# Moving part of the score sums and the output scaling between VectorE and ScalarE in a two-layer decode kernel

## The chip, the cores and the metric

The kernel runs on one core of one Trainium2 chip. The metric is the device time of one execution in microseconds (us). Every time that is read from a trace comes from one profiled execution and is counted from the start of its span. The engines are written as in the profile: PE is TensorE (PEld its weight loads), DVE is VectorE, ACT is ScalarE, POOL is GpSimd, and SPq is the queue of SyncE, from which nearly all loads are issued.

## The reference

One new token for each of two batch rows goes through an attention layer and a gated feed-forward layer, and then through both once more with the same weights and the same cache:

```python
B, Sq, D = 2, 1, 448;  H, Sk, Dh = 16, 4096, 256;  F = 1792
def _A_ref(x, k_cache, v_cache, wq, wo):
    q = (x @ wq).reshape(B, Sq, H, Dh).transpose(0, 2, 1, 3)
    scores = einsum("bhqd,bhkd->bhqk", q, k_cache) * (Dh ** -0.5)
    o = einsum("bhqk,bhkd->bhqd", softmax(scores), v_cache)
    return o.transpose(0, 2, 1, 3).reshape(B, Sq, H * Dh) @ wo
def _B_ref(x, W_gate, W_up, W_down):
    gate = x @ W_gate;  up = x @ W_up
    return (relu(gate) * up) @ W_down
x = x + _A_ref(layernorm(x), ...);  x = x + _B_ref(layernorm(x), ...)
x = x + _A_ref(layernorm(x), ...);  x = x + _B_ref(layernorm(x), ...)
```

All of it is float32. Keys and values of one head and one batch row are 4 MB each, so a pass over the cache reads nearly 270 MB.

## The kernel before

**Units and passes.** A unit is one head for one batch row, so a pass of attention has 32 units, numbered `u` from 0 to 31. The kernel has two passes, `attention(first, keep)` and `attention(second, ...)`, and behind each the feed-forward layer, `ffn(False)` and `ffn(True)`. A unit's keys are 128 partitions of 32 key rows ("tiles" `t`) of 256 numbers each, cut into four chunks `c` of 8 tiles; its values are cut in the same way.

**Loads and slots.** All weights, keys and values pass through one SBUF buffer, `arena`, of 27 slots of 1 MB. The list of loads is written out at the start. `pump` issues the next load from SyncE when a slot (or a block of 4 or 8 slots) is free; `release`, called behind the last reader of a slot, frees it and calls `pump`. Loads are issued in the list's order, so a load that has no slot holds up all behind it. In the middle of a pass one load brings 8 MB: the keys of unit `u` with the values of unit `u-1`. At the end of the first pass 20 chunks, the keys of units 29, 30 and 31 and the values of 30 and 31, together with one more chunk of values and one head's weights, stay in their slots, because the second pass begins with these units. While they stay, the remaining loads (7 of `w_in`, 4 of `w_out`, then the second pass) go through the five slots that are left.

**Scores.** The scores of a unit are products of its keys with the query, summed over 256 numbers. There are three ways of making them, and the first two appear in this case's edits.

- A block (`score_block`): VectorE multiplies all 32 tiles in place with one instruction (L378) and sums them with one (L386). Where `shared` is `CT` (8), ScalarE sums the first 8 tiles (L382) and VectorE the other 24. That is so for unit 0 of the first pass and for units from `ALONE` (25) on in both passes, and for three blocks early in the second pass.
- Kept keys (`score` with `kept`, units 29, 30 and 31 of the first pass): VectorE takes tile after tile with one instruction that multiplies and sums (L418, SCALAR_TENSOR_TENSOR). The products go to `junk`, a part of `down`, since the keys are wanted again.
- The rest, chunk by chunk, shared between VectorE and ScalarE (L409 to L418). Units 30 and 31 of the second pass are among these.

**Around the scores.** For each unit come the greatest score of a partition (`softmax_max`, L427 on VectorE and L429 on GpSimd), the exponentials (`softmax_exp`, L434 and L437 on ScalarE), the product with the values (`weigh`, L462 on TensorE), and the sum of its partial results in two steps: `out_copy` (L475, ScalarE) and `out_add` (L478, VectorE). `out_turn` (L488, TensorE) transposes the result, `out_keep` (L501, VectorE) scales it by the reciprocal of the softmax's sum for two units at once, and `project` (L511, TensorE) multiplies by `wo`. The order of a pass is the loop at the end of `attention`: in round `u` stand the scores of unit `u`, the weighing of unit `u-1` and the output of unit `u-2`. Each engine takes its instructions in that order. `query(u + 1)`, which makes the queries of two units, stands behind `project` in the rounds of odd `u`. For units 30 and 31 of the first pass the query stays in PSUM (`pq`), and TensorE makes it in round 29.

**The end.** In `ffn(True)` the output has four blocks of columns `c`, made from the four loads of `w_out`. The first three are gathered in `y_left`, copied by VectorE as one tile of 384 columns (L702) and written out by SyncE (L703); the last 64 columns go through `y_end` (L708 to L711) and are written by ScalarE's queue.

## Time and profile before

| | us |
|---|---|
| median of 3 runs (lowest, highest) | 1320.69 (1320.47, 1320.93) |
| the profiled execution, its own time | 1320.27 |
| its span | 1318.5 |
| busy in the span: DVE | 1081.6 (82%) |
| busy: PE | 553.7 (42%) |
| busy: ACT | 195.6 (15%) |
| busy: POOL | 269.0 (20%) |
| moved by DMA | 563.16 MB, 427 GB/s on average |

The time outside the span is 1320.27 - 1318.5 = 1.8 us. Shares of busy time are averages over stages: the middle of a pass, the turn from the first pass through `ffn(False)` to the second (about 570 to 760 us), and the end (from about 1220 us). In a row of the timeline stand start, duration, engine, line, operation, what is written and read, and in brackets how long the engine had been idle before it and what ended that.

### The profile page before, as it was taken

To read this page: it belongs to the slowest core of one execution; us is meant where nothing else is said; L and a number is where in the kernel's file an instruction comes from. 1 tells how busy PE (TensorE), PEld (TensorE's weight loads), DVE (VectorE), ACT (ScalarE), POOL (GpSimd) and SP (SyncE) were. 2 spreads that over 40 slices of the span, in tenths; PEclk is the share of its full clock that TensorE was granted. 3 is DMA by queue.
4 is the path that set the end of the run, shared out by engine and by line. 5 is a ranking of instruction groups with operands and counts; after the bars stand their busy time and mean duration, and the time that the engine had idled before them with its cause. 6 is when DMAs were issued, how large, how long until landed. Compare 5 with 4: busy or idle time off the path is not lost.

```text
span 1318.5 us, 9085 instructions
## 1 busy us (share of the span) xinstructions
PE 553.7 (42%) x3276; PEld 190.6 (14%) x3276; DVE 1081.6 (82%) x780; ACT 195.6 (15%) x776; POOL 269.0 (20%) x192
## 2 busy tenths in 40 slices
PE   2243342433434324345585444242433424434348
PEld 2011010110111101112141111110111101101113
DVE  4989888898888988888729987798888988877892
ACT  2100000000000000212026513000000000012241
POOL 0002003322133220321001153030123331230210
PEclk9675666656667667666697777666767667666679
DMA  9999999999999999999999999999999999999998
GB/s 408 435 430 429 432 428 437 432 436 434 417 445 435 430 430 426 445 418 430 421 405 416 431 430 435 438 432 430 432 431 436 433 428 436 429 432 425 427 425 334
DMA packets 22665, 563.16 MB, mean 427 GB/s; under 512 B 2520, under 2 KB 2652, under 8 KB 9564
## 3 DMA queue, kind: packets, MB, share of 16 engines
q1 hardware_dynamic: 22612, 562.57, 99.5%
q8 instruction: 26, 0.43, 0.1%
q14 instruction: 19, 0.16, 0.0%
q10 hardware_dynamic: 8, 0.00, 0.0%
HBM read 562.56 MB, written 0.00 MB: 427 GB/s over the span
## 4 chain that ended last, share of the span: by engine, by line
DMA 55%; DVE 32%; PE 7%; POOL 2%; issue 2%; ACT 1%; DVEq 0%; SPq 0%; POOLq 0%; ACTq 0%
DMA arena<-in_vk_dram 54%; DVE arena L378 12%; DVE scores L386 11%; DVE arena L409 3%; DVE down L418 2%; PE po L462 2%; POOL top L429 2%; DVE arena L418 2%; DMA arena<-in_w_out_dram 1%; DVE row L478 1%; PE small L488 1%; PE acc L511 1%; DVE scores L415 1%; ACT arena L411 1%; PE pf L576 1%
## 5 line engine op out<-in xcount | busy, mean ns | idle before, releaser
L378 DVE TENSOR_TENSOR arena<-arena 128x8192 f32<-128x8192 f32 x51 | 443.3, 8692 | 111.0 <-DMA arena<-in_vk_dram 110.9
L386 DVE TENSOR_REDUCE scores<-arena 128x32 f32<-128x8192 f32 (+1 forms) x53 | 431.8, 8148 | 0.0
L488 PE MATMUL small<-ones,row 128*128 128x1 f32 x256 | 62.0, 346 | 686.3 <-DVE row L478 686.3
L462 PE MATMUL po<-arena,probs 128*2 128x512 f32 x2048 | 303.1, 734 | 10.3 <-DMA arena<-in_vk_dram 6.6
L429 POOL PARTITION_ALL_REDUCE top<-mx x64 | 64.6, 1009 | 645.8 <-DVE mx L427 645.8
L443 POOL PARTITION_ALL_REDUCE total<-rs x64 | 176.1, 2752 | 61.3 <-ACT probs L437 60.3
L488 PEld LDWEIGHTS small<-ones,row 128*128 128x128 f32 x256 | 56.5, 308 | 748.9 <-DVE row L478 748.9
L434 ACT ACTIVATE nm<-top,nsr 128x1 f32<-128x1 f32 x64 | 18.8, 294 | 612.4 <-POOL top L429 612.4
L354 POOL PARTITION_BROADCAST arena<-arena x58 | 27.6, 545 | 300.6 <-ACT arena L350 300.6
L462 PEld LDWEIGHTS po<-arena,probs 128*2 128x2 f32 x2048 | 54.8, 96 | 198.3 <-issue 191.2
L338 PE MATMUL pq<-arena,xs 128*33 128x256 f32 x174 | 70.6, 571 | 14.1 <-DMA arena<-in_w_head_dram 14.1
L511 PE MATMUL acc<-arena,oT 128*2 128x448 f32 x128 | 50.9, 894 | 32.1 <-DVE oT L501 32.1
L350 ACT ACTIVATE arena<-pq 33x256 f32<-33x256 f32 x29 | 10.9, 377 | 321.7 <-PE pq L342 321.7
L382 ACT ACTIVATE arena<-arena 128x256 f32<-128x256 f32 x104 | 41.7, 402 | 86.2 <-DVE arena L378 86.2
L478 DVE SCALAR_TENSOR_TENSOR row<-po,lead,row 128x256 f32<-128x256 f32 x64 | 30.7, 479 | 25.8 <-ACT row L475 25.4
L411 ACT ACTIVATE arena<-arena 128x256 f32<-128x256 f32 x117 | 47.1, 404 | 20.4 <-DVE arena L409 20.1
L409 DVE TENSOR_TENSOR arena<-arena 128x1024 f32<-128x1024 f32 (+1 forms) x24 | 42.0, 1748 | 0.0
L338 PEld LDWEIGHTS pq<-arena,xs 128*33 128x33 f32 x174 | 25.3, 162 | 81.3 <-issue 66.7
L475 ACT ACTIVATE row<-po,lead 128x256 f32<-128x256 f32 x64 | 29.1, 455 | 21.2 <-PE po L462 21.2
L418 DVE SCALAR_TENSOR_TENSOR down<-arena,pq 128x256 f32<-128x256 f32 x64 | 26.9, 420 | 5.4 <-DMA arena<-in_vk_dram 3.4
L501 DVE TENSOR_TENSOR oT<-small,ri 128x4 f32<-128x4 f32 x32 | 5.1, 161 | 29.0 <-PE small L488 29.0
L437 ACT ACTIVATE probs<-scores,nm,sr 128x32 f32<-128x32 f32 x64 | 26.4, 413 | 2.1
(145 smaller groups left out, 359.0 us busy)
## 6 DMA issues: line engine op xcount, KB each, us to landing
arena<-in_vk_dram SPq DMA_DIRECT2D x16, 4096.0 KB, 40.0
arena<-in_w_head_dram SPq DMA_DIRECT2D x31, 896.0 KB, 30.9
arena<-in_vk_dram SPq DMA_DIRECT2D x27, 1024.0 KB, 14.9
arena<-in_vk_dram SPq DMA_DIRECT2D x12, 2048.0 KB, 38.5
arena<-in_w_in_dram SPq DMA_DIRECT2D x14, 896.0 KB, 26.2
arena<-in_w_out_dram SPq DMA_DIRECT2D x5, 896.0 KB, 8.9
arena<-in_vk_dram SPq DMA_DIRECT2D x47, 43.4
arena<-in_w_out_dram SPq DMA_DIRECT2D x1, 512.0 KB, 17.3
```

Of the source, the lines that this page charges most:

```text
L338: nc.tensor.matmul(q, xs[:, c, :], w[:, c * DH : (c + 1) * DH], start=(c == 0), stop=False)
L378: nc.vector.tensor_mul(kt, kt, q_of[u][:, None, :].to_broadcast([P, NT, DH]))
L386: nc.vector.reduce_sum(s_of[u][:, shared:], kt[:, shared:, :], axis=AX.X)
L409: nc.vector.tensor_mul(some, some, q_of[u][:, None, :].to_broadcast([P, whole, DH]))
L411: nc.scalar.activation(kt[:, t, :], kt[:, t, :], AF.Copy, accum_out=found[:, t : t + 1])
L418: nc.vector.scalar_tensor_tensor(junk if kept else kt[:, t, :], kt[:, t, :], 1.0, q_of[u], op0=ALU.mult, op1=ALU.mult, accum_out=found[:, ...
L429: nc.gpsimd.partition_all_reduce(mx_of[u], mx, P, RED.max)
L443: nc.gpsimd.partition_all_reduce(total[:, b : b + 1], rs, P, RED.add)
L462: nc.tensor.matmul(po_of[u][32 * t : 32 * t + 2, :], p_of[u][:, n : n + 2], vt[:, 2 * t * DH : (2 * t + 2) * DH], start=(c == 0), stop=(c ...
L478: nc.vector.scalar_tensor_tensor(row[:, :DH], po_of.pop(u)[:, DH:], lead[:, 1:2], row[:, :DH], op0=ALU.mult, op1=ALU.add,)
L488: nc.tensor.matmul(pT_of[u - u % 2][:, c, b : b + 1], row[:, c * P : (c + 1) * P], ones, start=True, stop=True,)
L511: nc.tensor.matmul(acc[at : at + B], oT_of[h][:, c, :], wo[:, c * D : (c + 1) * D], start=(n < 3), stop=(n >= n_u - 3),)
```

## The change

- In `score_block` ScalarE no longer takes 8 tiles at the end of a pass: VectorE sums all 32 tiles of units 25 to 28 of the first pass and 25 to 29 of the second.
- Of kept keys, tiles with odd `t` are multiplied by VectorE into `product` (the second half of `row`, one buffer for all of them) and summed by ScalarE. Even tiles stay as they were.
- `out_keep`'s multiplication for two units on VectorE becomes `out_scale`, an ACTIVATE for each unit on ScalarE. The one for an even unit is issued behind the reciprocal, that for an odd unit where `out_keep` stands.
- In `ffn(True)` the third block of output columns has its own PSUM tile, `y_third`. VectorE copies the first two blocks (256 columns), ScalarE the third.

```diff
-ALONE = 25
+    product = row[:, DH:]
@@ score_block
-            shared = 0 if (WHOLE_SECOND if ahead else WHOLE_FIRST)[0] <= u < ALONE else CT
+            shared = 0 if u >= (WHOLE_SECOND if ahead else WHOLE_FIRST)[0] else CT
@@ score
                 for t in range(whole, CT):
+                    if kept and t % 2:
+                        nc.vector.tensor_mul(product, kt[:, t, :], q_of[u])
+                        nc.scalar.activation(
+                            product, product, AF.Copy, accum_out=found[:, t : t + 1]
+                        )
+                        continue
                     nc.vector.scalar_tensor_tensor(
                         junk if kept else kt[:, t, :], kt[:, t, :], 1.0, q_of[u],
                         op0=ALU.mult, op1=ALU.mult, accum_out=found[:, t : t + 1],
@@ softmax_sum
             nc.vector.reciprocal(r_of[u - 1], total)
+            oT_of[order[u][0]] = work.tile([P, 2, B], F32, name="oT")
+            out_scale(u - 1)
@@ out_keep
+        def out_scale(u):
+            h, b = order[u]
+            share = r_of[u - u % 2][:, b : b + 1]
+            nc.scalar.activation(oT_of[h][:, :, b], pT_of[u - u % 2][:, :, b], AF.Copy, scale=share)
+
         def out_keep(u):
-            if u % 2 == 0:
-                return
-            h = order[u][0]
-            oT_of[h] = work.tile([P, 2, B], F32, name="oT")
-            share = r_of.pop(u - 1)[:, None, :].to_broadcast([P, 2, B])
-            nc.vector.tensor_mul(oT_of[h], pT_of.pop(u - 1), share)
+            if u % 2:
+                out_scale(u)
@@ ffn(True)
-            nc.tensor.matmul(y_left, unit, left, start=True, stop=False)
+            nc.tensor.matmul(y_left[:, : 2 * P], unit, left[:, : 2 * P], start=True, stop=False)
+            y_third = ps_s.tile([P, P], F32, name="small")[SUMS : SUMS + B]
+            nc.tensor.matmul(y_third, unit, left[:, 2 * P :], start=True, stop=False)
@@
                 if c > 0:
-                    to_y(before, False)
+                    to_y(before, c == FULL - 1)
                 before = at
+            nc.vector.tensor_copy(left[:, : 2 * P], y_left[:, : 2 * P])
             at = block(pds[FULL], FULL, range(14 - CLOSE))
             nc.scalar.activation(down[:, at], pds[FULL][:, at], AF.Copy)
-            to_y(before, True)
-            nc.vector.tensor_copy(left, y_left)
+            nc.tensor.matmul(y_third, scaled, down[:, before], start=False, stop=True)
+            nc.scalar.activation(left[:, before], y_third, AF.Copy)
             nc.sync.dma_start(found[:, : FULL * P], left)
```

The order of the instructions at three places follows; in brackets is what an instruction waits for (an engine's counter, or with DMAHW a load). First VectorE at the scores of unit 29, the first of the kept keys in the first pass, before the change:

```order
L418 SCALAR_TENSOR_TENSOR down,scores<-arena 128x256 [waits DMAHW6_49]
L418 SCALAR_TENSOR_TENSOR down,scores<-arena 128x256 [waits DVE_49] x7
L478 SCALAR_TENSOR_TENSOR row<-po,lead,row 128x256 [waits Activation_49]
L418 SCALAR_TENSOR_TENSOR down,scores<-arena 128x256 [waits DVE_49] x16
L501 TENSOR_TENSOR oT<-small,ri 128x4 [waits PE_49]
L418 SCALAR_TENSOR_TENSOR down,scores<-arena 128x256 [waits DVE_49] x8
```

And the first instructions of the same unit with the change:

```order
L424 SCALAR_TENSOR_TENSOR down,scores<-arena 128x256 [waits DMAHW6_49]
L419 TENSOR_TENSOR row<-arena 128x256
L424 SCALAR_TENSOR_TENSOR down,scores<-arena 128x256 [waits DVE_49]
L419 TENSOR_TENSOR row<-arena 128x256 [waits Activation_49]
L424 SCALAR_TENSOR_TENSOR down,scores<-arena 128x256 [waits DVE_49]
L419 TENSOR_TENSOR row<-arena 128x256 [waits Activation_49]
```

Every second instruction is now a product for ScalarE, and from the second product on each waits for ScalarE, which reads the one buffer; the L501 of this unit is gone from VectorE.

Second, ScalarE from the exponentials of unit 28 (L440 and L443) through unit 29's share to the exponentials of unit 29, with the change:

```order
L440 ACTIVATE nm<-top,nsr 128x1 [waits Pool_49]
L443 ACTIVATE probs,rs<-scores,nm,sr 128x32 [waits DVE_49,Activation_49]
L483 ACTIVATE row<-po,lead 128x256 [waits PE_49]
L420 ACTIVATE row,scores<-row 128x256 [waits DVE_49] x12
L506 ACTIVATE oT<-small,ri 128x2 [waits PE_49]
L420 ACTIVATE row,scores<-row 128x256 [waits DVE_49] x4
L440 ACTIVATE nm<-top,nsr 128x1 [waits Pool_49]
```

Between L483 (`out_copy` of unit 27) and the next L440 there was nothing before the change; now 16 sums (L420) stand there, the first of them behind `out_copy`, and `out_scale` (L506) of unit 27 stands behind the twelfth.

Third, VectorE at the end of the second pass, units 28 and 29, before the change:

```order
L386 TENSOR_REDUCE scores<-arena 128x24 [waits DVE_49]
L427 TENSOR_REDUCE mx<-scores 128x1 [waits DVE_49,Activation_49]
L378 TENSOR_TENSOR arena<-arena 128x8192 [waits DMAHW4_49]
L478 SCALAR_TENSOR_TENSOR row<-po,lead,row 128x256 [waits Activation_49]
L501 TENSOR_TENSOR oT<-small,ri 128x4 [waits PE_49]
L386 TENSOR_REDUCE scores<-arena 128x24 [waits DVE_49]
```

And with the change:

```order
L386 TENSOR_REDUCE scores<-arena 128x32 [waits DVE_49]
L433 TENSOR_REDUCE mx<-scores 128x1 [waits DVE_49]
L378 TENSOR_TENSOR arena<-arena 128x8192 [waits DMAHW4_49]
L486 SCALAR_TENSOR_TENSOR row<-po,lead,row 128x256 [waits Activation_49]
L386 TENSOR_REDUCE scores<-arena 128x32 [waits DVE_49]
```

Each sum (L386) now takes 32 tiles where it took 24, and L501, which waited for TensorE, no longer stands ahead of it.

## The prediction

> **What bounds the kernel now.** I read the page's span and DMA queues first, then the stretches of 4 us around the turn between the passes (columns: length, then busy time of PE, PEld, DVE, ACT and POOL, granted clock, DMA share, GB/s), then the timeline and the chain of waits there.
>
> ```profile
> span 1318.5 us, 9085 instructions
> q1 hardware_dynamic: 22612, 562.57, 99.5%
> ...
> 664.00:668.00 4.00, 3.54 (x25) 2.07 (x26) 1.07 (x6) 1.89 (x3) 0.00 (x0) 1.00 1.01 419
> 668.00:672.00 4.00, 3.90 (x37) 1.23 (x36) 0.94 (x6) 0.02 (x1) 0.00 (x0) 1.00 0.79 297
> ...
> 652.29 0.33 SPq L131 DMA_DIRECT2D arena<-in_w_in_dram  x1
> 669.46 0.33 SPq L131 DMA_DIRECT2D arena<-in_w_in_dram  x1
> ...
> 649.27 0.91 PE acc L511 x2
> 668.45 3.40 PE pf L576 x32
> ```
>
> The loads fill 99.5% of the span, so the bound is the transfer of 563 MB, and VectorE's work costs time only where it lets the queue run dry or delays what follows the last load. The queue runs dry in one place: at 668 to 672 us 297 GB/s stand where the stretch before has 419, a loss of (419 - 297) / 419 x 4 = 1.2 us. No load is issued between 652.29 and 669.46. The five free slots hold five loads of w_in, and the sixth waits until TensorE has used the first (L576, from 668.45). So the end of the first pass already sets when loads go on. **Whatever comes later there is added to the time in full.** TensorE's chain to that point runs from `project` of unit 29 (649.27), which waits for that unit's scaled output.
>
> **The part that decides: VectorE and ScalarE in units 27 to 31.** VectorE before the change (rows of the timeline), then the groups by form:
>
> ```profile
> 569.25 8.69 DVE L378 TENSOR_TENSOR arena<-arena 128x8192 f32<-128x8192 f32 x1 [4.05 <-DMA arena<-in_vk_dram]
> 579.44 0.16 DVE L501 TENSOR_TENSOR oT<-small,ri 128x4 f32<-128x4 f32 x1 [1.10 <-PE small L488]
> 596.93 6.53 DVE L386 TENSOR_REDUCE scores<-arena 128x24 f32<-128x6144 f32 x1
> 603.67 0.41 DVE L418 SCALAR_TENSOR_TENSOR down<-arena 128x256 f32<-128x256 f32 x1
> 604.13 0.42 DVE L418 SCALAR_TENSOR_TENSOR down<-arena 128x256 f32<-128x256 f32 x1
> 615.02 0.16 DVE L501 TENSOR_TENSOR oT<-small,ri 128x4 f32<-128x4 f32 x1
> 622.41 0.42 DVE L418 SCALAR_TENSOR_TENSOR down<-arena,pq 128x256 f32<-128x256 f32 x1 [3.36 <-DMA arena<-in_vk_dram]
> 637.70 0.19 DVE L427 TENSOR_REDUCE mx<-scores 128x1 f32<-128x32 f32 x1
> 649.06 0.16 DVE L501 TENSOR_TENSOR oT<-small,ri 128x4 f32<-128x4 f32 x1
> ...
> L386 DVE TENSOR_REDUCE scores<-arena 128x32 f32<-128x8192 f32 x40 | 346.8, 8671 | 0.0
> L386 DVE TENSOR_REDUCE scores<-arena 128x24 f32<-128x6144 f32 x13 | 85.0, 6538 | 0.0
> L409 DVE TENSOR_TENSOR arena<-arena 128x1024 f32<-128x1024 f32 x12 | 14.6, 1216 | 0.0
> L409 DVE TENSOR_TENSOR arena<-arena,pf 128x768 f32<-128x768 f32 x3 | 2.8, 949 | 0.0
> L411 ACT ACTIVATE arena<-arena 128x256 f32<-128x256 f32 x117 | 47.1, 404 | 20.4 <-DVE arena L409 20.1
> L434 ACT ACTIVATE nm<-top,nsr 128x1 f32<-128x1 f32 x64 | 18.8, 294 | 612.4 <-POOL top L429 612.4
> ```
>
> *Whole blocks on VectorE.* Each of units 25 to 28 costs 8.67 - 6.54 = 2.13 us more. In 25 and 26 the wait for the next keys takes it up (4.05 us of wait before unit 27's product, at 569.25). Unit 27 gains 1.10, the wait ahead of L501 that leaves VectorE, and so ends 2.13 - 1.10 = 1.03 late; unit 28, which waits for no load, adds 2.13. Unit 29 starts at 603.67 + 3.16 = 606.83.
>
> *Price of a shared pair of tiles.* No row has a product of 256 columns. From 949 and 1216 ns for 768 and 1024 columns a column costs 1.043 ns, so 256 take 0.949 - 512 x 0.001043 = 0.415 us. The hand-off is seen at the end of the second pass; the last row, of the chain of waits, has five of the sums on VectorE early in that pass, each with its read:
>
> ```profile
> 1281.80 2.28 DVE L409 TENSOR_TENSOR arena<-arena 128x2048 f32<-128x2048 f32 x1
> 1284.12 0.42 ACT L411 ACTIVATE arena<-arena 128x256 f32<-128x256 f32 x1 [1.81 <-DVE arena L409]
> 1285.33 0.40 ACT L411 ACTIVATE arena<-arena 128x256 f32<-128x256 f32 x1
> 1285.86 0.19 DVE L427 TENSOR_REDUCE mx<-scores 128x1 f32<-128x32 f32 x1 [0.52 <-ACT arena L411]
> ...
> 692.30 1.71 DVE arena L418 x10
> ```
>
> ScalarE starts 0.04 after VectorE's end (1284.08 to 1284.12), and VectorE goes on 0.53 after the start of ScalarE's last sum (1285.33 to 1285.86; the accumulator is read within it). With one `product` buffer the next product waits for the sum of the last, so a pair takes 0.415 + 0.04 + 0.53 = 0.98 us, whatever VectorE does in between. Two tiles on VectorE alone take 2 x 0.46 = 0.92 (603.67 to 604.13). The sharing makes a pair no shorter. Bounds: 0.68 if the buffer held nothing up, which is VectorE's own part (a sum that needn't wait for the last one takes 1.71 / 5 = 0.34, and the product between 256 x 0.001043 = 0.27 and 0.415, so 0.61 to 0.76); 0.86 if the buffer is free when ACTIVATE itself ends (0.40 after its start in L411); 1.06 if each hand-over took twice the 0.04 seen.
>
> *ScalarE's order.* A unit's first sum now stands behind `out_copy` of two units earlier:
>
> ```profile
> 605.07 0.45 ACT L475 ACTIVATE row<-po,lead 128x256 f32<-128x256 f32 x1
> 622.00 3.62 PE L462 MATMUL po<-arena,probs 128*2 128x512 f32 x32
> 625.68 0.47 ACT L475 ACTIVATE row<-po,lead 128x256 f32<-128x256 f32 x1 [5.24 <-PE po L462]
> 639.17 0.45 ACT L475 ACTIVATE row<-po,lead 128x256 f32<-128x256 f32 x1
> ```
>
> - Unit 29: ScalarE is free 605.52 - 603.67 = 1.85 after the unit's start, so its first sum starts at 608.68 and its twelfth 11 x 0.98 = 10.8 later, at 619.46. Behind that comes `out_scale` of unit 27: 0.40 for the sum, and 0.29 for an ACTIVATE with a per-partition scale (L434), so 620.15 instead of 615.18 (615.02 + 0.16). That is **5.0 late**. `project` and the query of units 30 and 31 follow on TensorE, so unit 30 starts at 627.4 instead of 622.41.
> - Unit 30: `out_copy` waits for the weighing of unit 28 (622.00 to 625.62), which stands behind that query. It ends at 626.15 + 5.0 = 631.1, and only then the first sum starts; VectorE stands still meanwhile with its second product. The sixteenth starts 14.7 later, and the greatest score follows at 645.8 + 0.53 = 646.4 instead of 637.70: 8.7 late.
> - Unit 31: ScalarE is free at 639.62 + 8.7 = 648.3; twelfth sum at 659.1, `out_scale` done at 659.8 instead of 649.22. **10.5 late**, and with it `project`, the weighings and L576.
>
> The queue meanwhile stays empty, so the loads go on 10.5 us later. Nothing else hides it: the five slots are full.
>
> **The end.** In the second pass units 25 to 27 hide their sums again; units 28 and 29 don't:
>
> ```profile
> 1220.97 8.69 DVE L378 TENSOR_TENSOR arena<-arena 128x8192 f32<-128x8192 f32 x1 [4.51 <-DMA arena<-in_vk_dram]
> 1236.79 8.68 DVE L378 TENSOR_TENSOR arena<-arena 128x8192 f32<-128x8192 f32 x1
> 1280.60 0.42 ACT L411 ACTIVATE arena<-arena 128x256 f32<-128x256 f32 x1 [1.75 <-DVE arena L409]
> 1281.73 0.15 DVE L501 TENSOR_TENSOR oT<-small,ri 128x4 f32<-128x4 f32 x1
> 1312.10 0.96 PE L669 MATMUL pf<-arena,row 128*32 128x128 f32 x26 [0.17 <-DMA arena<-in_w_out_dram]
> 1314.17 0.52 PE L669 MATMUL po<-arena,row 128*32 128x128 f32 x10 [0.30 <-DMA arena<-in_w_out_dram]
> 1314.98 0.47 PE L669 MATMUL pf<-arena,row 128*32 128x64 f32 x18 [0.17 <-DMA arena<-in_w_out_dram]
> 1316.49 0.26 ACTq L711 DMA_DIRECT2D out_dram<-row  x1
> ```
>
> Before unit 28 there are 4.51 us of waiting, before unit 29 none. So VectorE is 2.13 + 2.13 - 1.10 = 3.16 late against the loads. `out_scale` of unit 29 stands on ScalarE behind four sums that start at 1280.60: with 0.40 for each and 0.29 it ends at 1282.5, where L501 ended at 1281.88, 0.6 more. TensorE comes to `w_out` 3.7 late. Its waits for those loads are 0.17 + 0.30 + 0.17 = 0.64 in these rows; counting gaps between its weight loads too, I take 1.0 as cover, so 2.7 stay (bounds 2 to 3.1). The copies of y in parts shorten SyncE's path alone; the other output leaves last (1316.49), so they bring 0 to 0.25, and I take 0.2.
>
> Outputs scaled on ScalarE cost or bring nothing else: in the middle of a pass the wait for L501 (1.1 in odd units) goes, but VectorE then waits longer for keys.
>
> **Sum**, against the profiled execution: 1320.3 + 10.5 + 2.7 - 0.2 = 1333.3. Its own time is 0.4 under the median of the runs; I forecast **1333**, 0.9% slower.
>
> **A rule against this.** In units 29 to 31 VectorE's sums follow each other without a pause while ScalarE waited 5.24 us before one `out_copy`. The Trainium skill, Perfetto Trace Analysis, "Optimizing Scalar/DVE Operations", says that with a saturated DVE handing work to Scalar may make sense. By that rule the first rival below would come out, 1322; the row at 1285.86, where VectorE waits 0.52 for ScalarE's sum, speaks for the hand-off as the limit instead.
>
> **Rivals.** The three units hold 11 + 15 + 11 = 37 pairs on the path, so each 0.01 us of the pair is 0.37 us.
> - *The hand-off doesn't limit; not slower.* Place: the one product buffer in units 29 to 31. At 0.68 a pair the delay of 10.5 shrinks by 37 x 0.30 = 11.1, to -0.6, and with the end's 2.5 the time is 1322.2, no change. It decides below 0.70 us a pair. For it: VectorE's own part is that short. Against it: one buffer, and 0.53 from a sum's start to its release. 5%.
> - *The buffer comes free with ACTIVATE itself*, 0.86: 37 x 0.12 = 4.4 less, 1328.9. Against it: the wait of 0.52 for the last sum. 12%.
> - *The loads hide the later turn*: only the end's 2.5, 1322.8. For it: the queue is 99.5% busy. Against it: nothing was in flight at 670. 5%.
> - *It is worse*: TensorE at a lower granted clock in the longer pauses, or 1.06 a pair (37 x 0.08 = 3.0): 1336 to 1338. 14%.
> - *Faster*: 2%; the empty queue gives back 1.2 at most. Forecast itself: 62%.
>
> **Numbers.** About 0.2% (2.6 us) is what this measurement can tell from no change. The two cases at 1322 to 1323 are within it, 9 to 10% with their neighbours; faster 2%; slower 88%. The forecast's own range is 1330 to 1336; with the early release and the worse case it is 1326 to 1338.
>
> **What would show it.** The stretch at 668 to 682 us with next to no GB/s; the sixth load of w_in issued near 680 instead of 669.5; L419 followed by the next L419 after 0.98; L424 and L419 idle for some 3 us at the start of unit 30, ended by ScalarE; units 25 to 27 waiting 2 us less for keys. The forecast is wrong if L419's pace is under 0.8, if loads are issued between 653 and 679, or if w_out's products (L680) wait for loads as before.

## The result and the profile after

| | before | after |
|---|---|---|
| median of 4 runs each (lowest, highest), us | 1320.62 (1320.47, 1320.93) | 1333.97 (1332.19, 1335.04) |
| the profiled execution, its own time, us | 1320.27 | 1335.04 |
| its span, us | 1318.5 | 1332.6 |

The change makes the kernel 13.35 us slower: ratio 1.0099, 95% interval 1.0083 to 1.0115. The profiled execution of after is its slowest run, 1.07 over the median, which matters below where single microseconds at the end are counted.

The page of after, its span and its queue of loads (packets, MB, share of 16 engines' span):

```profile
span 1332.6 us, 9006 instructions
q1 hardware_dynamic: 22612, 562.57, 98.5%
```

The same 562.57 MB, but the queue is no longer as good as full. Where it stands empty is seen in the stretches of 4 us around the turn (length, busy time of PE, PEld, DVE, ACT and POOL, granted clock, DMA share, GB/s):

```profile
664.00:668.00 4.00, 3.57 (x30) 1.36 (x24) 0.74 (x3) 1.68 (x6) 0.73 (x2) 1.00 0.99 410
668.00:672.00 4.00, 4.00 (x34) 1.17 (x38) 0.00 (x0) 0.26 (x1) 0.00 (x0) 1.00 0.49 201
672.00:676.00 4.00, 3.68 (x22) 1.11 (x15) 0.48 (x1) 0.73 (x2) 0.00 (x0) 1.00 0.00 2
676.00:680.00 4.00, 3.71 (x32) 1.85 (x32) 1.65 (x10) 1.91 (x3) 0.00 (x0) 1.00 0.00 0
680.00:684.00 4.00, 4.00 (x40) 1.51 (x36) 0.44 (x3) 0.70 (x2) 0.00 (x0) 1.00 0.79 266
```

Against 419 GB/s the four stretches from 668 lose (218 + 417 + 419 + 153) / 419 x 4 = 11.5 us, where the kernel before lost 1.2. These are 10.3 of the 14.1 us by which the span grew. The chain that ends the gap, from the timeline of after (SyncE's load, ScalarE's scaling of units 27 and 29, TensorE's `project` of unit 29 and its first product with `w_in`):

```profile
619.64 0.24 ACT L506 ACTIVATE oT<-small,ri 128x2 f32<-128x2 f32 x1
660.33 0.24 ACT L506 ACTIVATE oT<-small,ri 128x2 f32<-128x2 f32 x1
660.62 0.91 PE L520 MATMUL acc<-arena,oT 128*2 128x448 f32 x2 [7.25 <-ACT oT L506]
678.88 3.21 PE L585 MATMUL pf<-arena,xs 128*32 128x448 f32 x32
679.89 0.33 SPq L130 DMA_DIRECT2D arena<-in_w_in_dram  x1
```

The sixth load of `w_in` is issued at 679.89 instead of 669.46, since the first `w_in` product comes at 678.88 instead of 668.45: both 10.43 late. `project` of unit 29 is 11.35 late (649.27 before), so TensorE made up 0.9 on the way. The scaled output of unit 27 came at 619.88 instead of 615.18.

What held VectorE up in units 29 and 30, from the timeline of after:

```profile
606.31 0.19 DVE L433 TENSOR_REDUCE mx<-scores 128x1 f32<-128x32 f32 x1
606.41 0.42 DVE L424 SCALAR_TENSOR_TENSOR down<-arena 128x256 f32<-128x256 f32 x1
606.75 0.42 DVE L419 TENSOR_TENSOR row<-arena 128x256 f32<-128x256 f32 x1
608.70 0.42 DVE L419 TENSOR_TENSOR row<-arena 128x256 f32<-128x256 f32 x1 [1.18 <-ACT row L420]
609.15 0.42 ACT L420 ACTIVATE row<-row 128x256 f32<-128x256 f32 x1 [0.49 <-DVE row L419]
609.70 0.42 DVE L419 TENSOR_TENSOR row<-arena 128x256 f32<-128x256 f32 x1 [0.23 <-ACT row L420]
627.58 0.42 DVE L424 SCALAR_TENSOR_TENSOR down<-arena,pq 128x256 f32<-128x256 f32 x1 [3.62 <-PE pq L317]
631.15 0.47 ACT L483 ACTIVATE row<-po,lead 128x256 f32<-128x256 f32 x1 [5.81 <-PE po L470]
632.05 0.42 DVE L419 TENSOR_TENSOR row<-arena,pq 128x256 f32<-128x256 f32 x1 [3.37 <-ACT row L420]
647.07 0.19 DVE L433 TENSOR_REDUCE mx<-scores 128x1 f32<-128x32 f32 x1 [0.57 <-ACT row L420]
```

The row at 609.70 shows the lock step: a product of 0.42, ScalarE's sum 0.45 after the product's start, and 0.55 from the sum's start to the next product, 1.00 us a pair, with both engines idle in every pair (0.23 on VectorE, 0.49 on ScalarE). The rows at 608.70 and 632.05 show the second product of units 29 and 30 waiting 1.18 and 3.37 for the first sum, which stands behind `out_copy` (L483; for unit 30 the row at 631.15). Unit 30 ends 9.4 late (637.70 before).

The groups by form (busy us and mean ns of one; idle before and what ended it) show the block sums and ScalarE's share of the kept tiles in after:

```profile
L386 DVE TENSOR_REDUCE scores<-arena 128x32 f32<-128x8192 f32 x49 | 424.9, 8671 | 0.0
L386 DVE TENSOR_REDUCE scores<-arena 128x24 f32<-128x6144 f32 x4 | 26.1, 6537 | 0.0
L420 ACT ACTIVATE row<-row 128x256 f32<-128x256 f32 x48 | 20.0, 416 | 21.7 <-DVE row L419 21.7
```

Nine sums have gone from 24 to 32 tiles (13 and 40 of them before), each 2.13 dearer, and ScalarE is idle 21.7 us before its 48 sums, waiting for products.

The end, from the timeline of after: unit 28's product, the greatest scores of unit 31, the last part of the weighing of unit 30, its `out_copy`, and the last issue.

```profile
1231.70 8.69 DVE L378 TENSOR_TENSOR arena<-arena 128x8192 f32<-128x8192 f32 x1 [4.36 <-DMA arena<-in_vk_dram]
1299.35 0.19 DVE L433 TENSOR_REDUCE mx<-scores 128x1 f32<-128x32 f32 x1 [0.52 <-ACT arena L411]
1300.07 3.28 PE L470 MATMUL po<-arena,probs 128*2 128x512 f32 x17
1303.42 0.47 ACT L483 ACTIVATE row<-po,lead 128x256 f32<-128x256 f32 x1 [2.50 <-PE po L470]
1330.68 0.26 ACTq L723 DMA_DIRECT2D out_dram<-row  x1
```

Unit 28 starts 10.7 late, which is the turn; unit 31's scores are 13.5 late (1285.86 before) and the last issue 14.2 (1316.49 before). Behind the turn 3.7 us more are lost in this execution.

### The profile page after: what moved, and what is told of

It reads as the page before. It is cut to its first block, busy times and chain, and to the rows that moved or that the text cites. A ratio compares the mean times of both kernels' runs of the same rounds, so it can differ in the third digit from the quotient of the medians.

```text
span 1332.6 us, 9006 instructions
## 1 busy us (share of the span) xinstructions
PE 561.2 (42%) x3278; PEld 190.3 (14%) x3278; DVE 1091.5 (82%) x700; ACT 206.1 (15%) x793; POOL 269.7 (20%) x192
## 3 DMA queue, kind: packets, MB, share of 16 engines
q1 hardware_dynamic: 22612, 562.57, 98.5%
## 4 chain that ended last, share of the span: by engine, by line
DMA 51%; DVE 27%; PE 12%; POOL 4%; ACT 4%; issue 3%; DVEq 0%; SPq 0%; POOLq 0%; ACTq 0%
DMA arena<-in_vk_dram 51%; DVE arena L378 11%; DVE scores L386 9%; POOL top L435 4%; PE po L470 4%; DVE arena L409 3%; PE acc L520 2%; PE pq L338 2%; DVE arena L424 1%; ACT row L420 1%; DVE row L419 1%; ACT arena L411 1%; DVE row L486 1%; PE pf L585 1%; PE small L496 1%
## 5 line engine op out<-in xcount | busy, mean ns | idle before, releaser
L386 DVE TENSOR_REDUCE scores<-arena 128x32 f32<-128x8192 f32 (+1 forms) x53 | 451.0, 8510 | 0.0
L470 PE MATMUL po<-arena,probs 128*2 128x512 f32 x2048 | 315.6, 759 | 4.4 <-ACT probs L443 4.4
L435 POOL PARTITION_ALL_REDUCE top<-mx x64 | 72.7, 1136 | 664.0 <-DVE mx L433 663.9
L449 POOL PARTITION_ALL_REDUCE total<-rs x64 | 168.7, 2636 | 61.3 <-ACT probs L443 61.3
L506 ACT ACTIVATE oT<-small,ri 128x2 f32<-128x2 f32 x64 | 16.5, 258 | 521.8 <-PE small L496 521.8
L338 PE MATMUL pq<-arena,xs 128*33 128x256 f32 x174 | 67.7, 549 | 15.0 <-DMA arena<-in_w_head_dram 15.0
L440 ACT ACTIVATE nm<-top,nsr 128x1 f32<-128x1 f32 x64 | 18.8, 294 | 352.9 <-POOL top L435 352.9
L411 ACT ACTIVATE arena<-arena 128x256 f32<-128x256 f32 x117 | 47.1, 404 | 20.3 <-DVE arena L409 20.0
L483 ACT ACTIVATE row<-po,lead 128x256 f32<-128x256 f32 x64 | 29.2, 456 | 21.2 <-PE po L470 21.2
L443 ACT ACTIVATE probs<-scores,nm,sr 128x32 f32<-128x32 f32 x64 | 26.4, 413 | 2.2
L420 ACT ACTIVATE row<-row 128x256 f32<-128x256 f32 x48 | 20.0, 416 | 21.7 <-DVE row L419 21.7
L419 DVE TENSOR_TENSOR row<-arena,pq 128x256 f32<-128x256 f32 x32 | 13.4, 420 | 10.6 <-ACT row L420 10.6
```

The source lines that it names most:

```text
L338: nc.tensor.matmul(q, xs[:, c, :], w[:, c * DH : (c + 1) * DH], start=(c == 0), stop=False)
L386: nc.vector.reduce_sum(s_of[u][:, shared:], kt[:, shared:, :], axis=AX.X)
L411: nc.scalar.activation(kt[:, t, :], kt[:, t, :], AF.Copy, accum_out=found[:, t : t + 1])
L420: nc.scalar.activation(product, product, AF.Copy, accum_out=found[:, t : t + 1])
L435: nc.gpsimd.partition_all_reduce(mx_of[u], mx, P, RED.max)
L449: nc.gpsimd.partition_all_reduce(total[:, b : b + 1], rs, P, RED.add)
```

## The experiments

Theory: the turn is late by its block sums, by the pace of the one product buffer, and by the first sums' place behind `out_copy`; the end is late by its block sums. The rivals blame one part alone: the scaling on ScalarE, the block sums, or the hand-over to ScalarE whatever the buffers. Each run was timed beside the kernel before on the same chip (medians 1320.64 to 1320.71).

The table has every run. "Turn" is the start of the first `w_in` product in the profiled execution less 668.45; "end" is what its span has over 1318.5 beyond that. Both come from one execution of each kernel: e12, which changes nothing before the end, has a turn of 0.45, and e9, whose first pass is that of after, one 0.66 later than after's, so differences of the turn below some 0.7 say nothing.

| kernel | median, us | ratio to before (95%) | turn | end |
|---|---|---|---|---|
| after | 1333.97 | 1.0099 (1.0083 to 1.0115) | 10.43 | 3.7 |
| e1: no kept sharing | 1323.47 | 1.0019 (1.0010 to 1.0028) | 0.36 | 2.9 |
| e2: block sums back | 1329.47 | 1.0066 (1.0051 to 1.0081) | 9.99 | -0.2 |
| e3: scaling on VectorE | 1333.49 | 1.0097 (1.0082 to 1.0112) | 10.02 | 2.7 |
| e4: three buffers | 1322.34 | 1.0013 (1.0004 to 1.0023) | 0.15 | 1.7 |
| e5: sharing from the second chunk | 1328.16 | 1.0054 (1.0038 to 1.0069) | 5.96 | 2.1 |
| e6: kept sharing alone | 1325.88 | 1.0038 (1.0025 to 1.0052) | 5.79 | -0.4 |
| e7: three buffers, block sums back | 1321.46 | 1.0007 (0.9998 to 1.0016) | 0.05 | 0.6 |
| e8: as e7, scaling on VectorE | 1320.24 | 0.9996 (0.9987 to 1.0005) | 0.44 | -0.9 |
| e9: block sums back, second pass | 1330.93 | 1.0074 (1.0061 to 1.0088) | 11.09 | -0.5 |
| e10: block sums alone | 1327.01 | 1.0046 (1.0032 to 1.0060) | 3.56 | 2.5 |
| e11: scaling on ScalarE alone | 1321.98 | 1.0009 (1.0000 to 1.0018) | 0.28 | 1.0 |
| e12: y in parts alone | 1320.57 | 0.9999 (0.9990 to 1.0008) | 0.45 | 0.0 |

Every run, from after to e12, holds y in parts.

### e1: the change without the kept sharing

```diff
-                    if kept and t % 2:
-                        nc.vector.tensor_mul(product, kt[:, t, :], q_of[u])
-                        nc.scalar.activation(
-                            product, product, AF.Copy, accum_out=found[:, t : t + 1]
-                        )
-                        continue
```

> The change with its kept tiles all on VectorE again (block sums on VectorE to the end of a pass, outputs scaled on ScalarE and y in parts stay). Theory (the three units' shared pairs and what stands behind them on ScalarE make the turn late): a pair takes 0.92 again, out_scale of unit 27 no longer stands behind sums, TensorE reaches the first w_in at 668.5 or a little before, the queue loses at most 1.2 us there, and only the end's 2 to 3.8 stay: 1322.5 to 1324.5. Rival 1 (the block sums of units 27 and 28 alone make the turn late): first w_in 2.7 late or more, 1326 to 1328. Rival 2 (scaling on ScalarE is itself the cause): first w_in stays near 679, 1330 or more.

1323.47: 10.5 of the 13.35 are gone, as the theory has it. From e1's timeline, ScalarE's scaling of unit 27 and TensorE's first `w_in`:

```profile
611.52 0.26 ACT L500 ACTIVATE oT<-small,ri 128x2 f32<-128x2 f32 x1 [3.34 <-PE small L490]
668.81 3.21 PE L579 MATMUL pf<-arena,xs 128*32 128x448 f32 x32
```

With no sums ahead of it the scaling waits for TensorE alone (3.34 us, for L490, `out_turn`) and comes at 611.52, earlier than VectorE's 615.02 before the change. So although unit 29 still starts 2.7 late, the turn keeps its time. With the outputs scaled on ScalarE, the turn loses nothing unless pairs are shared.

### e2 and e9: block sums shared again, in both passes and in the second alone

```diff
+ALONE = 25
-            shared = 0 if u >= (WHOLE_SECOND if ahead else WHOLE_FIRST)[0] else CT
+            shared = 0 if (WHOLE_SECOND if ahead else WHOLE_FIRST)[0] <= u < ALONE else CT
```

and, for e9, in place of the last line:

```diff
+            shared = 0 if (WHOLE_SECOND[0] <= u < ALONE if ahead else u >= WHOLE_FIRST[0]) else CT
```

> The change with eight block sums of units 25 to 28 on ScalarE again, in both passes. Theory (block sums are 2.7 of the turn's 10.4 and about 2.7 of the end's 3.8): unit 29 starts near 603.7, first w_in near 676, 1328 to 1330.5. Rival 1 (they alone make the turn late): first w_in near 668.5, about 1321. Rival 2 (they only take up slack): 1333 to 1334.

> The change with eight block sums of units 25 to 28 on ScalarE again in the second pass only. Theory (the end's part is mostly these sums; the turn isn't touched): first w_in stays near 678.9, the end gives back 2.5 to 3.8: 1330 to 1331.5. Rival (what the end lost beyond the turn is TensorE's lower clock in the weighing of unit 30, whatever the sums): 1333 or more.

e2's total, 1329.47, is in the theory's range and 4.50 under after. e9, with the sums back in the second pass alone, has 3.04 of these. The other 1.46 (1330.93 - 1329.47) are what the first pass's sums cost beside the shared pairs, where the theory had 2.7. In the profiled execution of e2 even less is seen: its first `w_in` was to come at 676 and came at 678.44. The timeline of e2 (`project` of unit 29, first `w_in`):

```profile
658.79 0.91 PE L521 MATMUL acc<-arena,oT 128*2 128x448 f32 x2 [7.25 <-ACT oT L507]
678.44 3.21 PE L586 MATMUL pf<-arena,xs 128*32 128x448 f32 x32
```

`project` comes 1.83 earlier than in after (660.62), not 2.7. The scaling on ScalarE stands behind eight block sums again, and unit 29 starts at 605.17 where the kernel before had 603.67. Of the 1.83 TensorE then gives back 1.4: from `project` to `w_in` it takes 19.65 in e2, 18.26 in after, 19.18 before. The stretches of 2 us show why, after first, then e2 (the third number from the end is the granted clock):

```profile
662.00:664.00 2.00, 2.00 (x14) 0.53 (x10) 1.39 (x6) 1.02 (x5) 0.00 (x0) 0.57 1.04 430
664.00:666.00 2.00, 2.00 (x24) 0.88 (x19) 0.18 (x1) 1.20 (x5) 0.35 (x1) 1.00 0.99 409
```

```profile
662.00:664.00 2.00, 2.00 (x17) 0.90 (x15) 0.21 (x2) 1.14 (x5) 0.35 (x1) 0.50 0.99 409
664.00:666.00 2.00, 2.00 (x16) 0.51 (x9) 0.00 (x0) 0.17 (x2) 0.39 (x1) 0.82 1.03 420
```

TensorE starts 1.83 earlier in e2, yet its clock goes up 1 us later. That belongs to these two executions: in the profiled one of e9 the clock goes up later still and the first `w_in` comes at 679.54, 1.1 after e2's. The medians, 1.46 apart, are the better measure. So two thirds of what e2 gains lie at the end (e9, with a turn no earlier than after's) and one third at the turn. Over all runs the end costs 1.7 to 3.7 where block sums of the second pass are on VectorE (after, e1, e3, e4, e5, e10) and -0.9 to 1.0 where they are shared.

### e3: outputs scaled by VectorE again

```diff
-            oT_of[order[u][0]] = work.tile([P, 2, B], F32, name="oT")
-            out_scale(u - 1)
@@ out_keep
-            if u % 2:
-                out_scale(u)
+            if u % 2 == 0:
+                return
+            h = order[u][0]
+            oT_of[h] = work.tile([P, 2, B], F32, name="oT")
+            share = r_of.pop(u - 1)[:, None, :].to_broadcast([P, 2, B])
+            nc.vector.tensor_mul(oT_of[h], pT_of.pop(u - 1), share)
```

> The change with the outputs scaled by one VectorE product per pair of units again. Theory (the scaling only waits with VectorE and ScalarE, which go in lock step, and costs 0.6 at the end at most): first w_in within 0.7 of 678.9, 1333 to 1335. Rival (ScalarE's place for out_scale, behind the sums, is the cause of the late project): out_scale of unit 27 back near 615 to 617, first w_in 5 to 10 earlier, 1323 to 1329.

1333.49, and the scaling of unit 27 comes at 620.38, no earlier than on ScalarE:

```profile
620.38 0.15 DVE L512 TENSOR_TENSOR oT<-small,ri 128x4 f32<-128x4 f32 x1
678.47 3.21 PE L587 MATMUL pf<-arena,xs 128*32 128x448 f32 x32
```

The rival falls: with the two engines in lock step it doesn't matter on which of them the scaling waits.

### e4: three product buffers

```diff
-    product = row[:, DH:]
+    spare = row[:, DH:]
@@ score
+                        n = (c * CT + t) // 2 % 3
+                        product = spare if n == 0 else ps_f.tile([P, DH], F32, name="pf")
                         nc.vector.tensor_mul(product, kt[:, t, :], q_of[u])
```

> The change with three product buffers in turn (the old one and two in PSUM), so that a product no longer waits for the sum before it. Theory (the one buffer sets the pace of 1.00 us a pair and the stalls of 1 to 3.4 us at a unit's start): a pair takes 0.65 to 0.76, units 29 to 31 end at or before their old times although unit 29 still starts 2.7 late, first w_in at 668.5 or before, and the end's 2.5 to 3.8 stay: 1322.5 to 1324.5. Rival (handing tiles to ScalarE costs VectorE or ScalarE the 1.00 whatever the buffers, by contention or by ScalarE's own time for a sum): pair above 0.9, first w_in at 675 or later, 1330 to 1334.

1322.34, just under the range (1322.5). The timeline of e4 in unit 29, two products in a row, and the first `w_in`:

```profile
609.77 0.42 DVE L421 TENSOR_TENSOR pf<-arena 128x256 f32<-128x256 f32 x1
610.11 0.42 DVE L426 SCALAR_TENSOR_TENSOR down<-arena 128x256 f32<-128x256 f32 x1
610.45 0.43 DVE L421 TENSOR_TENSOR pf<-arena 128x256 f32<-128x256 f32 x1
668.60 3.31 PE L587 MATMUL pf<-arena,xs 128*32 128x448 f32 x32
```

A pair takes 0.68, and VectorE doesn't stand idle in it. That was the prediction's lower bound, and with it the whole loss at the turn is gone, with nothing changed but where the products go. The one buffer, not the work handed over, was the price. Two of the three buffers lie in PSUM, and no run has a single buffer there; but a sum from PSUM is only 0.05 shorter (the last section), which can't make up the 0.32 between 1.00 and 0.68. What stays is the end's.

### e5: sharing from a unit's second chunk on

```diff
-                    if kept and t % 2:
+                    if kept and c > 0 and t % 2:
```

> The change with the sharing of kept tiles begun only at a unit's second chunk: the first eight tiles stay on VectorE, so the first product comes 3.7 us into the unit, when ScalarE is through with out_copy. The one buffer stays. Theory (the stalls at the starts of units 29 to 31, 1.2, 3.4 and about 1 us in the changed kernel, are a large part of the turn's 10.4, since 1.00 a pair instead of 0.93 makes only 37 x 0.07 = 2.6): the stall of 3.4 at unit 30 falls under 0.6, first w_in at 672.5 to 675 instead of 678.9, 1327.5 to 1330.5. Rival (the pace alone counts, the stalls only move): 12 of 16 pairs still at 1.00, first w_in at 678 or later, 1333 or more.

1328.16. In e5's timeline VectorE goes through unit 30's first chunk (from 625.54) without a wait for a sum; the only wait for ScalarE there is 0.41 for `out_copy` itself:

```profile
629.62 0.48 DVE L486 SCALAR_TENSOR_TENSOR row<-po,lead,row 128x256 f32<-128x256 f32 x1 [0.41 <-ACT row L483]
630.36 0.41 DVE L419 TENSOR_TENSOR row<-arena,pq 128x256 f32<-128x256 f32 x1
674.41 3.21 PE L585 MATMUL pf<-arena,xs 128*32 128x448 f32 x32
```

Starting the sharing 8 tiles later takes 4.5 us off the turn. Of the 37 pairs 12, four in each unit, also went from 1.00 to 0.92, which is 12 x 0.08 = 1.0 of the 4.5. So the stalls at the starts, which are a matter of ScalarE's order, were worth some 3.5, a third of the turn's 10.43.

### e6, e10, e11 and e12: each part alone

Each is the change with the other parts undone: e6 has the edits of e2 and e3, e10 those of e1 and e3, e11 those of e1 and e2, e12 all three. Against the kernel before, e12 is the edit of `ffn(True)` alone, and e6, e10 and e11 add to it, in this order:

```diff
+                    if kept and t % 2:
+                        nc.vector.tensor_mul(product, kt[:, t, :], q_of[u])
+                        nc.scalar.activation(
+                            product, product, AF.Copy, accum_out=found[:, t : t + 1]
+                        )
+                        continue
```

```diff
-            shared = 0 if (WHOLE_SECOND if ahead else WHOLE_FIRST)[0] <= u < ALONE else CT
+            shared = 0 if u >= (WHOLE_SECOND if ahead else WHOLE_FIRST)[0] else CT
```

```diff
@@ softmax_sum
+            oT_of[order[u][0]] = work.tile([P, 2, B], F32, name="oT")
+            out_scale(u - 1)
@@ out_keep
+            if u % 2:
+                out_scale(u)
```

> The kernel before with only the sharing of the kept tiles over one product buffer (and y in parts): block sums on both engines and outputs scaled by VectorE as before. Theory: unit 29 starts at 603.7 to 604 as before, pairs take 1.00, unit 30's first sum again stands behind out_copy, first w_in 5 to 8 late, nothing at the end: 1326 to 1328.6. Rival 1 (what the change lost at the turn with block sums in place, e2's 1329.5 less the end, is all the sharing's): 1329 or more. Rival 2 (sharing alone doesn't hurt; it needs the late start of unit 29): within 0.2% of before, 1318 to 1323.

> The kernel before with only the block sums on VectorE to the end of a pass (and y in parts): no sharing of kept tiles, outputs scaled by VectorE. Theory: units 27 and 28 add 2.1 each less what waits take up, and without out_scale on ScalarE the 1.10 before L501 stays, so unit 29 starts near 607.6 as in e3; unit 30's query waits for the scaling of unit 27 on VectorE in the middle of unit 29, so the turn is as late as that start, 3 to 4, and the end 2.5 to 3.5: 1325.5 to 1328. Rival (where the outputs are scaled doesn't matter, the turn keeps its time as in e1): 1322.5 to 1324.

> The kernel before with only the outputs scaled on ScalarE (and y in parts): block sums shared, kept tiles on VectorE. Theory: out_scale of an even unit behind eight block sums comes later than on VectorE, unit 29 starts 0.6 to 1.6 late, but nothing stands ahead of out_scale of unit 27, so the turn keeps its time; at the end 0.6 less cover: 1320.2 to 1321.6. Rival (it is the scaling that makes the turn late): 1323 or more.

> The kernel before with only y copied in parts. Theory (the output on the other queue leaves last): 1320.3 to 1320.9, a gain of 0 to 0.25 that can't be told from none. Rival (SyncE's output set the end): 1319.5 to 1320.2.

Sharing alone costs 5.2 us (0.1 less than the low end expected), all of it at the turn. Block sums alone cost 6.3, of which 3.6 at the turn. Scaling on ScalarE costs 1.3, a little more than expected and at the edge of what can be told from nothing, with a turn 0.28 late, so at the end. The traces show where: in the second pass `out_scale` of unit 27 stands on ScalarE behind eight block sums and starts at 1250.35 (L501 of e11), where VectorE's scaling in e12 stands at 1249.02 (L507), and `project` of unit 29 comes at 1283.69 instead of 1282.45. y in parts brings nothing that can be measured. The four add up to 5.2 + 6.3 + 1.3 - 0.1 = 12.7 of the 13.35, but that they nearly do is partly chance: e1, which holds the second and the third, costs 2.8 and not 7.6.

The timeline of e10 (VectorE's scaling of unit 27, first `w_in`) beside e1's shows how the third part works on the second:

```profile
619.10 0.16 DVE L506 TENSOR_TENSOR oT<-small,ri 128x4 f32<-128x4 f32 x1
672.01 3.21 PE L581 MATMUL pf<-arena,xs 128*32 128x448 f32 x32
```

On VectorE the scaling stands behind 24 tiles of a unit that starts late, 619.10; on ScalarE, without shared pairs, it comes at 611.52 and the turn's 3.56 fall to 0.36. The scaling on ScalarE would have paid for the block sums at the turn, had the shared pairs not been put ahead of it.

### e7 and e8: what could be kept

e7 is e2 and e4 together; e8 has VectorE's scaling (e3) as well, so that of the change only the sharing, over three buffers, and y in parts are left.

```diff
+ALONE = 25
-    product = row[:, DH:]
+    spare = row[:, DH:]
+                        product = spare if n == 0 else ps_f.tile([P, DH], F32, name="pf")
```

> Three product buffers, block sums of units 25 to 28 shared again; outputs scaled on ScalarE and y in parts stay. Theory (the turn can't come earlier than the last values' arrival and the steps behind it let it, about 1.2 us of empty queue in both kernels; the end is as before): 1319.8 to 1321.3, no change that can be told from before. Rival (scaling on ScalarE behind the shared block sums makes units 28 and 29 late, as e2's start of unit 29 at 605.2 hints, and costs at the end): 1321.5 to 1322.5.

> As the run before it, with the outputs scaled on VectorE again: what stays of the change is the sharing of kept tiles, over three buffers, and y in parts. Theory: the shared pairs take 0.68, units 29 to 31 end some 8 us of VectorE's time earlier in sum, but the queue's loss at the turn stays at 1.2 to 1.5 us since the values of unit 31 come no earlier, and y in parts brings 0 to 0.25: 1319.6 to 1321. Rival (the turn follows VectorE's end in the kernel before too): the loss at 668 to 672 us goes, 1319.0 to 1319.6, about 0.1% faster.

e7 came out at 1321.46, between the two expectations: no change that can be told from before, with a median 0.16 over the theory's range and 0.04 under the rival's, so that it decides for neither. e8, without the scaling on ScalarE, is at 1320.24, no difference from before either, but 1.2 under e7. That is what e11 showed: with the block sums shared, the scaling on ScalarE costs some 1.2 to 1.3. e8's stretch at the turn, and from its timeline VectorE's start of unit 30 and TensorE's last part of the weighing of unit 31:

```profile
668.00:672.00 4.00, 3.91 (x41) 1.56 (x41) 1.32 (x9) 0.47 (x1) 0.00 (x0) 1.00 0.73 258
```

```profile
622.46 0.42 DVE L427 SCALAR_TENSOR_TENSOR down<-arena,pq 128x256 f32<-128x256 f32 x1 [6.55 <-DMA arena<-in_vk_dram]
662.56 1.04 PE L471 MATMUL po<-arena,probs 128*2 128x512 f32 x8 [0.60 <-DMA arena<-in_vk_dram]
```

VectorE spends 37 x 0.24 = 9 us less on the pairs that lay on the path, and the queue still loses (419 - 258) / 419 x 4 = 1.5 us. Why nothing is won: VectorE waits 6.55 for unit 30's keys, which come no earlier than before (622.41 there), and TensorE waits for the last values of unit 31. From those to the first `w_in` it takes 6.33 (668.89 - 662.56), as before (6.34, 668.45 - 662.11). So in the kernel before, the work on units 29 to 31 was at the edge of mattering: a later scaled output delays the turn (e6, e10), an earlier one brings nothing. No version here beats the kernel before by more than can be measured.

## Why the prediction was right, and where it wasn't

Forecast 1333, measured 1333.97; the mechanism and the place were right, and some sizes were off in both directions. In the profiled execution, for which the sum was made, the span grew by 14.1 where the sum adds 13.0 (10.5 + 2.7 - 0.2), and TensorE's clock in point 5, 1.2, is as large as the difference.

1. *The loads bound the kernel, and what comes later at the turn is added in full.* Right: the queue stands empty until the sixth `w_in` load, 10.43 late, and nothing of it is made up later.
2. *Block sums: unit 29 starts 3.16 late.* Measured 2.74 (606.41 against 603.67). L501's own 0.16 was left out of what unit 27 gains, unit 27's keys came 0.1 earlier, and up to the next instruction a sum of 32 tiles costs 2.06 more, not 2.13 (586.86 - 578.15 against 586.17 - 579.52). A step that the forecast took for granted is wrong: that this delay is simply part of the turn's 10.5. e1 has the same late start and a turn on time, and in the medians of e2 and e9 the first pass's sums cost 1.5 beside the shared pairs. What they cost at the turn depends on where the scaling stands and what stands ahead of it (e1 and e10).
3. *A pair costs 0.98.* Measured 1.00, by the steps named: product, hand-over, and the next product only behind the sum's accumulator read. e4 shows both the mechanism and the lower bound of 0.68.
4. *ScalarE's order.* `out_scale` of unit 27 at 619.88 (forecast 620.15), unit 30's start 627.58 (627.4), its greatest scores 647.07 (646.4), `out_scale` of unit 29 done at 660.57 (659.8). The last is 0.8 later than forecast, and the loads were not, because TensorE took 0.9 less from there to `w_in`: two errors that cancelled, so that the turn's 10.43 is as near to 10.5 by luck. Unit 30's start came out in the same way. In the kernel before the unit waited for its keys, as the forecast's own row says (3.36, ended by a load), and its query was through 0.34 earlier, at 622.07 (L317: 621.46 + 0.61). With the change the query took 0.77 longer from `project` on (619.94 to 627.54 against 615.24 to 622.07): in the stretches of 2 us the granted clock goes up 6.2 behind `project` there, 4.7 before. e5 shows that the stalls at the units' starts were real and worth some 3.5 us.
5. *The end: 3.7 late, 1.0 covered, 2.7 left, y -0.2: 2.5.* The profiled execution lost 3.7, the medians 13.35 - 10.43 = 2.9. e9 puts 3.0 on the second pass's block sums. `project` of unit 29 came 3.7 late against the turn, as forecast (1296.07 - 1281.94 = 14.1, less 10.43), but TensorE came to `w_out` 5.0 late (1326.25 - 1310.86 = 15.4). None of its products there waits for a load any more, so the cover was used up, and it was 1.2 (5.0 less the last issue's 3.8) instead of 1.0. The term that was mis-sized in that execution is the weighing of unit 30: from its first part to `out_copy` it took 1303.42 - 1296.08 = 7.3 us, where before it was 1288.11 - 1282.05 = 6.1. The granted clock went up 3.5 behind that first part before (at 1285.5, (0.62 - 0.50) / 0.50 x 2 = 0.5 ahead of 1286) and 5.9 behind it with the change (at 1302); the rows stand below the list. 2.4 us more at half the clock are the 1.2. That mechanism stood among the worse rivals. The forecast also said that scaling on ScalarE costs nothing but 0.6 for `out_scale` at the end. That holds with the block sums on VectorE (e3, 0.5 between the medians); with the sums shared it costs some 1.2 to 1.3 (e11; e7 less e8).
6. *y in parts: 0 to 0.25.* e12: none that can be measured.

The stretches of 2 us for point 5, of before and then of after (the third number from the end is the granted clock):

```profile
1284.00:1286.00 2.00, 2.00 (x17) 0.77 (x12) 1.45 (x3) 1.71 (x8) 0.00 (x0) 0.62 0.97 397
```

```profile
1300.00:1302.00 2.00, 2.00 (x15) 0.68 (x11) 0.00 (x0) 0.80 (x3) 0.44 (x2) 0.50 1.03 422
1302.00:1304.00 2.00, 1.90 (x13) 0.35 (x5) 0.07 (x1) 0.47 (x1) 0.00 (x0) 1.00 1.01 416
```

**The rivals.** The hand-off not limiting (1322) and the early release of the buffer (0.86 a pair) fall with the pace of 1.00. That the loads hide the turn falls with the empty stretch. The Trainium skill's advice to hand work from a saturated DVE to Scalar (Perfetto Trace Analysis, "Optimizing Scalar/DVE Operations") brought no time here. With one buffer the pair became longer. With three it went from 0.92 to 0.68, but two sums on VectorE alone also take 0.68 where neither waits for the other (the last section), and the total stayed the same (e8).

## What to carry to other kernels

Work handed tile by tile to another engine can pay only if the buffer between them holds more than one tile: work out a pair's round trip (product, hand-over, sum, release) and compare it with doing both on one engine before anything else. Ask first why the one engine takes as long as it does; here a quarter of its time for a tile (0.12 of 0.46) was a wait for the instruction before it. Look at what already stands on the receiving engine's queue, since the first tile handed over waits behind it and so does everything that is queued behind the tiles. Where a kernel is bound by loads, go by the place where the queue runs dry: earlier work buys nothing there, later work is paid in full.

## What was not expected of the hardware

TensorE's granted clock went from 0.50 to 1.00 at very different times after it began to work without a pause. From the shares in the stretches of 2 us: in after `project` starts at 660.62 and the clock is up 0.28 before 664 ((0.57 - 0.50) / 0.50 x 2), 3.1 later; in e2 it starts at 658.79 and the clock is up at 664.7, 5.9 later. Two executions of the same instructions differ as much: e9, whose first pass is that of after, starts at 659.99 and has the clock up at 665.7 (0.58 in the stretch from 664), 5.7 later. The 2.8 between the first two are worth 1.4 us at half the clock on a chain of 19, enough to hide most of e2's gain at the turn in these executions. The Trainium skill, TensorE: Matmul & The Clock Gate, "Part 1: The HAM clock gate", says that the clock follows activity in windows that run freely, so the moment depends on where in a window the work begins. The runs agree that it isn't tied to the work's start, though they spread more widely than the half microsecond to either side that the Trainium skill gives there.

VectorE's instruction that multiplies and sums stands 0.46 behind the last one in units 29 to 31 of the kernel before (603.67, 604.13). Early in the second pass of the same kernel it stands 0.34 behind it:

```profile
688.62 0.42 DVE L418 SCALAR_TENSOR_TENSOR arena<-arena,pf 128x256 f32<-128x256 f32 x1 [0.66 <-PE pf L725]
688.96 0.41 DVE L418 SCALAR_TENSOR_TENSOR arena<-arena,pf 128x256 f32<-128x256 f32 x1
```

It is the same line (L418). What differs is where the products go: back into the keys' own place here, and into `junk`, the same place for all of them, when the keys are kept, so that each waits for the last; the first order list above has this wait on VectorE's own counter. (A query in PSUM isn't the difference: unit 30 has one too, and its first two stand 0.47 apart, 622.41 and 622.88.) With a plain product between two of them the wait doesn't show (610.11 to 610.45 in e4). So the 0.24 that a pair gains in e4 is twice this wait of 0.12, and handing a sum to ScalarE would not be needed for it. That is read from the lists and the paces; no run gives the kept products two places in turn without sharing.

Sums on ScalarE were quicker from PSUM than from SBUF, from e4's groups by form (mean ns last but one):

```profile
L422 ACT ACTIVATE pf<-pf 128x256 f32<-128x256 f32 x30 | 11.0, 368 | 5.4 <-DVE pf L421 5.4
L422 ACT ACTIVATE row<-row 128x256 f32<-128x256 f32 x18 | 7.4, 413 | 2.0 <-DVE row L421 1.7
```

368 against 413 ns, for the same 256 columns.
